# Causal attention and an MLP on one core: the score matmuls of a pair in one group, and another table of engines and ranks for the planner

## The chip, the cores and the metric

The kernel runs on one core of a Trainium2 chip. The time is the device time of one execution in us; smaller is better. A core has TensorE (PE, matmuls, with its weight loads shown apart as PEld), VectorE (DVE), ScalarE (ACT), GpSimd (POOL) and SyncE (SP), which here issues all DMAs. Each engine works through a queue of its own in order.

## The reference

```python
scores = q @ k.T / 8                      # q, k, v: 4 batches, 12 heads, 448 rows, 64 columns
scores = where(causal mask, -1e9, scores)
attn = exp(scores - max) / (sum + 1e-9)
x = (attn @ v) as (1792, 768)             # rows of all batches, heads side by side
h = x @ w_in                              # (768, 2048)
out = (h - tanh(h)) @ w_out               # (2048, 768)
```

The weights w_in and w_out come as 64-bit floats and are decoded on the chip.

## The kernel before, in words

**Numbers.** Nearly every operand of a matmul is split into two 16-bit parts, hi and lo, and three products (hi hi, hi lo, lo hi) are summed. `split` (L410) makes the parts: `scaled` (L396) writes hi = src * s, and a second step writes lo = src * s - hi. Either step can stand on VectorE (one pass for lo), or on GpSimd (for lo two passes: src scaled in place, then a subtraction); hi also on ScalarE.

**Stages.** (1) The first 128 rows of every batch are computed apart in `first_rows` (L595), with 32-bit matmuls: once for batches 0 and 1 (rank c0), once for batches 2 and 3 (rank c0b). (2) `w_in_chunk` (L445) loads and decodes w_in in 8 chunks. (3) `mlp_g` (L553) runs the MLP's first layer for these two groups of rows, 16 blocks of 18 matmuls each (`mlp1`, L519), chunk by chunk as w_in arrives; tanh on ScalarE, the rest of the eviction on VectorE, then a split into g. (4) `w_out_half` (L469) loads, decodes and splits the two halves of w_out. The second layer (`mlp2`, L535: 48 matmuls, one eviction o, one store) needs all of its half. (5) For each of the 4 batches `attention` (L735) computes the other 320 rows, and then the MLP runs on them. A batch has 6 pairs of heads. For a pair, `prep` (L654) loads q and k, bounds and splits q, k and v; query tile 0 has 256 keys, tile 1 has 384, and a last half tile of 64 rows has 448.

**Scores.** `weights_unit` (L684) handles one of the tiles 0 and 1 of a pair: 6 matmuls into two of four score banks (both heads, three products), for each head a VectorE pass that adds the mask and takes the minimum, an exponential on ScalarE with its sum, the reciprocal (`inverse`, L581), the split of the weights into p16 (tags p and p_lo, p_first for batch 0), and a DMA transpose into pT. `weights_last` (L702) does the same for the half tile, for two pairs at once. `values` (L723) multiplies with v: 54 matmuls for a pair into the bank b_x, which `split_x` empties into x. x has 9 buffers, so the attention can be three pairs ahead of the first layer of the batch before.

**Order.** Nothing is issued when it is written down: `Work` (L25 and on) collects all operations with the buffers that they touch, `schedule` (L159) lays them out by a list schedule with estimated costs (`cost`, L118) and waits, and `emit` (L228) issues them in order of their estimated start; so all instructions carry the line L232. Among the operations that an engine could start, the one with the lowest rank goes first. The ranks come from the table RANK; matmuls of the MLP have 10 and more, by batch and block. Operations that can stand on several engines are made by `either` (L107): its tag has a string in the table CFG, whose letters (V VectorE, A ScalarE, G GpSimd) are taken in turn. For example, "VAVV" for p puts three of four first halves of the weights on VectorE.

**The shared port.** The planner takes GpSimd's passes and some of VectorE's as users of one port, and doesn't let them overlap in its plan. In `add` (L70) VectorE's passes count if they read two large SBUF operands, or if they are a `tensor_scalar` with one, output of the same type and no scalar column.

**Buffers that tie the stages.** v of batch 0 lands where the x of the first rows was, and q and k of batch 0 land in the slot TS[4], which the second half of w_out uses last. The banks of the weights' decoding join the two score banks once w_out is done (`bank_s.bufs += banks[2:4]`).

## Time and profile before

| what | us |
|---|---|
| median of 3 runs (lowest, highest) | 605.71 (604.11, 606.19) |
| the profiled execution's own time | 603.75 |
| its span, first instruction to last | 602.0 |

A group of rows gives for each kind of instruction how often it ran, how long the engine was busy with it, the mean of one, and the idle time just before. The stretches are counted from the span's start. A busy TensorE means that matmuls overlap without a hole in the records; their ends are modelled. Names are the program's: b_s score banks, b_m the MLP's banks, b_x the banks of values, prob the exponentials, pn the split weights and pt their transposes, slot the large shared buffers, first a block that holds first rows, later g of batches 2 and 3, and later still second buffers of q, k, weights and exponentials.

### The profile page before, as it was taken

To read this page: it belongs to the slowest core of one execution; us is meant where nothing else is said; L and a number is where in the kernel's file an instruction comes from. 1 tells how busy PE (TensorE), PEld (TensorE's weight loads), DVE (VectorE), ACT (ScalarE), POOL (GpSimd) and SP (SyncE) were. 2 spreads that over 40 slices of the span, in tenths; PEclk is the share of its full clock that TensorE was granted. 3 is DMA by queue.
4 is the path that set the end of the run, shared out by engine and by line. 5 is a ranking of instruction groups with operands and counts; after the bars stand their busy time and mean duration, and the time that the engine had idled before them with its cause. 6 is when DMAs were issued, how large, how long until landed. Compare 5 with 4: busy or idle time off the path is not lost.

```text
span 602.0 us, 13635 instructions
## 1 busy us (share of the span) xinstructions
PE 559.2 (93%) x5144; PEld 375.9 (62%) x5144; DVE 451.6 (75%) x1286; ACT 294.8 (49%) x796; POOL 312.9 (52%) x389
## 2 busy tenths in 40 slices
PE   3688689999999999999999999999999999999997
PEld 3456468876555556765666666665666566776664
DVE  3889997989999999999959999921999961332000
ACT  5899899983366755553436463400644430121000
POOL 3577962883232157886528788510687820465000
PEclk9999899999999999999999999999999999999999
DMA  8995467645386974448563556640334281000100
GB/s 283 327 337 186 141 196 212 188 127 222 95 164 142 181 164 79 80 99 181 119 141 72 106 123 174 128 74 27 84 60 79 42 146 43 13 2 1 27 27 26
DMA packets 113378, 74.02 MB, mean 123 GB/s; under 512 B 89760, under 2 KB 99488, under 8 KB 112800
## 3 DMA queue, kind: packets, MB, share of 16 engines
q1 hardware_dynamic: 113312, 73.15, 48.8%
q8 instruction: 40, 0.66, 0.5%
q14 instruction: 26, 0.21, 0.1%
HBM read 45.61 MB, written 5.51 MB: 85 GB/s over the span
## 4 chain that ended last, share of the span: by engine, by line
PE 31%; DVE 31%; issue 3%; DMA 3%; POOL 3%; ACT 1%; DVEq 0%; SPq 0%; POOLq 0%; ACTq 0%
PE b_m L232 29%; DVE pn L232 6%; DVE prob L232 6%; DVE small L232 5%; DVE first L232 3%; DVE t L232 3%; DVE g L232 2%; PE b_x L232 2%; DVE v L232 2%; DVE k L232 1%; DMA e<-in_v_dram 1%; DVE x L232 1%; DMA slot<-in_qk_dram 1%; POOL g L232 1%; DMA pt<-pn 1%
## 5 line engine op out<-in xcount | busy, mean ns | idle before, releaser
L232 PE MATMUL b_m<-x,w_in 128*128 128x320 f16 (+1 forms) x1728 | 230.1, 291 | 15.3 <-DVE t L232 14.2
L232 PEld LDWEIGHTS <-w_in 128*128 128x128 f16 x1728 | 167.5, 98 | 72.1 <-issue 22.9
L232 PE MATMUL b_m<-slot,g 128*128 128x384 f16 x1152 | 192.4, 326 | 0.0
L232 PEld LDWEIGHTS <-g 128*128 128x128 f16 x1152 | 110.7, 98 | 74.9 <-issue 3.9
L232 ACT ACTIVATE prob<-prob,small 128x256 f32<-128x256 f32 (+2 forms) x102 | 58.8, 577 | 70.0 <-DVE small L232 69.5
L232 POOL TENSOR_SCALAR t<-t,small 128x320 f32<-128x320 f32 (+1 forms) x80 | 53.4, 668 | 51.6 <-DVE g L232 43.9
L232 ACT ACTIVATE t<-b_m,small 128x320 f32<-128x320 f32 (+1 forms) x96 | 48.1, 502 | 63.7 <-PE b_m L232 53.6
L232 DVE SCALAR_TENSOR_TENSOR t<-b_m,small,t 128x320 f32<-128x320 f32 (+1 forms) x96 | 49.9, 520 | 30.2 <-ACT t L232 30.0
L232 DVE TENSOR_SCALAR o<-b_m,small 128x384 f32<-128x384 f32 x28 | 17.1, 610 | 70.3 <-PE b_m L232 70.2
L232 POOL TENSOR_TENSOR g<-t,g 128x320 f16<-128x320 f32 x64 | 54.2, 847 | 5.3
L232 DVE CUSTOM_DVE_ANT_0 prob<-b_s,mask,small 128x384 f32<-128x384 f32 (+1 forms) x87 | 46.1, 545 | 0.2
L232 DVE SCALAR_TENSOR_TENSOR slot<-b_s,e 128x384 int32<-128x384 int32 x64 | 34.6, 547 | 5.5 <-ACT b_s L232 3.2
L232 DVE SCALAR_TENSOR_TENSOR pn<-prob,small,pn 128x256 f16<-128x256 f32 (+2 forms) x60 | 37.5, 645 | 0.1
L232 PEld LDWEIGHTS <-v 128*64 128x64 f16 x1296 | 31.5, 111 | 8.2 <-issue 8.0
L232 PE MATMUL b_m<-slot,first 128*128 128x384 f16 x192 | 33.6, 326 | 0.0
L232 PEld LDWEIGHTS <-first 128*128 128x128 f16 (+2 forms) x282 | 21.7, 98 | 17.6 <-issue 6.2
L232 PE MATMUL b_s<-k,q 64*128 64x256 f16 (+2 forms) x342 | 30.7, 317 | 0.4 <-DVE small L232 0.3
L232 ACT ACTIVATE e<-slot 128x768 f32<-128x768 f32 (+1 forms) x30 | 26.3, 876 | 5.4 <-DMA slot<-in_moe_w_in_dram 3.5
L232 POOL TENSOR_SCALAR prob<-prob,small 128x384 f32<-128x384 f32 (+2 forms) x24 | 15.4, 640 | 24.5 <-DVE pn L232 16.3
L232 DVE TENSOR_SCALAR g<-t,small 128x320 f16<-128x320 f32 x48 | 27.1, 564 | 0.4
L232 PE MATMUL b_x<-pt,v 128*64 128x64 f16 (+1 forms) x1026 | 26.3, 207 | 0.3 <-DMA pt<-pn 0.3
L232 DVE TENSOR_SCALAR small<-small 128x1 f32<-128x1 f32 (+4 forms) x159 | 26.0, 178 | 0.2
(137 smaller groups left out, 815.9 us busy)
## 6 DMA issues: line engine op xcount, KB each, us to landing
slot<-in_moe_w_in_dram SPq DMA_DIRECT2D x16, 768.0 KB, 6.2
slot<-in_qk_dram SPq DMA_DIRECT2D x18, 384.0 KB, 3.3
slot<-in_moe_w_out_dram SPq DMA_DIRECT2D x8, 768.0 KB, 4.7
e<-in_moe_w_out_dram SPq DMA_DIRECT2D x8, 768.0 KB, 4.5
e<-in_v_dram SPq DMA_DIRECT2D x3, 1536.0 KB, 6.6
out_dram<-o SPq DMA_DIRECT2D x24, 192.0 KB, 1.9
first<-in_qk_dram SPq DMA_DIRECT2D x6, 384.0 KB, 3.4
g<-in_qk_dram SPq DMA_DIRECT2D x6, 256.0 KB, 6.5
```

Of the source, the lines that this page charges most:

```text
L232: getattr(self.eng[o["eng"]], method)(*args, **kw)
```

## The change

It has four parts. `weights_units` replaces `weights_unit`: at tile 0 all 12 matmuls of the pair's tiles 0 and 1 are issued as one group into four score banks, and the passes on tile 1 use the banks later. `split` gets a third way for lo: ScalarE scales src in place and GpSimd subtracts; and the two passes of GpSimd's way become two operations of the plan. The plan's costs and its port change: every VectorE `tensor_scalar` with one large SBUF input and no PSUM operand counts as a user, an operation may start 190 or 135 ns before the port is free, the port stays taken 75 or 22 ns longer, some passes of ScalarE cost 75 ns more and GpSimd's subtraction 20 ns. And the tables CFG and RANK are other ones: of the ranks, c0b goes from 9.316 to -12.684, evac from 4.208 to -4.596, w_out from 7.476 to -4.564, att from -0.165 to -7.342, w_in from -12.778 to -17.446, c0 from -14.292 to -74.72, att0 from -13.314 to -11.803.

```diff
@@ -97,23 +97,28 @@
         if eng == "G":
             shared = bool(ins)
         else:
-            two_ports = method == "tensor_scalar" and len(big) == 1 and outs[0].dtype == big[0].dtype and len(ins) == 1
+            two_ports = method == "tensor_scalar" and len(big) == 1 and not any(x.space == bass.MemoryType.PSUM for x in outs + ins)
             shared = eng == "V" and (len(big) > 1 or two_ports)
         op.setdefault("shared", set()).update([eng] if shared else [])
         cost, move = self.cost(eng, method, outs, ins)
         total[0] += cost
         op["move"] += move
 
-    def either(self, tag, *ways):
+    def either(self, tag, *ways, again=False, A="A"):
 
         self.ops.append(dict(alts={}, deps=set(), rank=self.rank, move=0.0))
         self.alt = True
         for f in ways:
             f()
         self.alt = None
-        n = self.turn[tag] = self.turn.get(tag, -1) + 1
-        way = CFG[tag]
-        self.ops[-1].update(eng=way[n % len(way)], tag=(tag, n))
+        n = self.turn[tag] = self.turn.get(tag, -1) + (not again)
+        way = CFG[tag].replace("A", A)
+        self.ops[-1].update(eng=way[n % len(way)], tag=(tag, n), A=A)
+
+    def nothing(self, eng):
+        self.ops[-1]["alts"][eng] = [], [0.0]
+        self.ops[-1].setdefault("shared", set())
 
     def cost(self, eng, method, outs, ins):
         o = max(outs, key=lambda x: x.size())
@@ -135,10 +140,11 @@
             b = o.size() * mybir.dt.size(o.dtype)
             return 540.0, b / (360.0 if run >= 512 else 180.0)
         if eng == "A":
-            return n * 0.833 + (51 if psum else 94) + 93 * aps + 93 * (len(outs) > 1), 0.0
+            words = ins[0].space != bass.MemoryType.PSUM and (o.space == bass.MemoryType.PSUM or ins[0].ap[-1][0] > 1)
+            return n * 0.833 + (51 if psum else 94) + 93 * aps + 93 * (len(outs) > 1) + 75 * (words and not aps), 0.0
         if eng == "G":
             if method == "tensor_tensor":
-                return n * 1.885 + 148, 0.0
+                return n * 1.885 + 168, 0.0
             return n * 0.83 + 245, 0.0
         if method in ("tensor_scalar", "tensor_copy") and not psum and not any(st == 0 for x in ins for st, m in x.ap[1:] if m > 1):
             return n * 0.52 + 70 + 60 * aps, 0.0
@@ -179,7 +185,8 @@
                 heapq.heappush(ready[e], (self.ops[i]["rank"], i))
             _, i = heapq.heappop(ready[e])
             o = self.ops[i]
-            if e in o["shared"] and port > t:
+            lead = 190.0 if e == "V" else 135.0
+            if e in o["shared"] and port - lead > t:
                 other = [x for x in ready[e] if e not in self.ops[x[1]]["shared"]]
                 if other:
                     heapq.heappush(ready[e], (o["rank"], i))
@@ -200,8 +207,8 @@
                 else:
                     turn, mode = self.TURN, o["mode"]
             if e in o["shared"]:
-                t = max(t, port)
-                port = t + o["cost"]
+                t = max(t, port - lead)
+                port = t + o["cost"] + (75.0 if e == "V" else 22.0)
             o["start"] = t
             end = t + turn + o["cost"]
             if e == "T":
@@ -219,7 +226,7 @@
             for j in users[i]:
                 left[j] -= 1
                 f = self.ops[j]["eng"]
-                at[j] = max(at[j], end + (self.SAME if f == e else self.LAT)[f])
+                at[j] = max(at[j], end + (self.LAT[f] if f != e else self.SAME[f] if o["cost"] else 0.0))
                 if not left[j]:
                     heapq.heappush(waiting[f], (at[j], j))
         self.span = max(free.values())
@@ -409,12 +416,11 @@
 
     def split(hi, lo, src, s, tag):
 
-        def lo_pool():
-            G.tensor_scalar(src, src, s, 1.0, ALU.mult, ALU.mult)
-            G.tensor_tensor(lo, src, hi, ALU.subtract)
-
         scaled(hi, src, s, tag)
-        wk.either(tag + "_lo", lambda: V.scalar_tensor_tensor(lo, src, s, hi, ALU.mult, ALU.subtract), lo_pool)
+        wk.either(tag + "_lo", lambda: wk.nothing("V"), lambda: G.tensor_scalar(src, src, s, 1.0, ALU.mult, ALU.mult),
+                  lambda: A.activation(src, src, AF.Copy, scale=s))
+        wk.either(tag + "_lo", lambda: V.scalar_tensor_tensor(lo, src, s, hi, ALU.mult, ALU.subtract),
+                  lambda: G.tensor_tensor(lo, src, hi, ALU.subtract), again=True, A="G")
@@ -681,23 +687,27 @@
         S.dma_start_transpose(out=pT.rearrange("p x a t q -> p (x a t) q"), in_=p16.rearrange("p x a k -> p (x a k)"))
         return pT
 
-    def weights_unit(b, o, i):
-        w = W[i]
+    def weights_units(b, o, n):
+        if n == 0:
+            o.pS = [[bank_s() for _ in range(2)] for _ in range(2)]
+            with wk.group():
+                for i in range(2):
+                    w = W[i]
+                    for m, (x, y) in enumerate(HL):
+                        for h, half in enumerate(halves):
+                            T.matmul(o.pS[i][h][:, :w], o.q[half, x, i * P:(i + 1) * P], o.k[half, y, :w], start=(m == 0), stop=(m == 2))
+        w = W[n]
         total, mn = r_sum(), r_mn()
-        pS = [bank_s(), bank_s()]
-        with wk.group():
-            for n, (x, y) in enumerate(HL):
-                for h, half in enumerate(halves):
-                    T.matmul(pS[h][:, :w], o.q[half, x, i * P:(i + 1) * P], o.k[half, y, :w], start=(n == 0), stop=(n == 2))
         es = [e_ring()[:, :w] for _ in range(2)]
         for h in range(2):
-            softmax_part(es[h], pS[h][:, :w], mask[:, 3 * P - w:], o.cn, mn[:, h:h + 1], total[:, h:h + 1])
+            softmax_part(es[h], o.pS[n][h][:, :w], mask[:, 3 * P - w:], o.cn, mn[:, h:h + 1], total[:, h:h + 1])
         inverse(total, 2.0 ** -14)
-        p16 = p16_rings[i]()
+        p16 = p16_rings[n]()
         for h in range(2):
             split(p16[:, h, 0, :], p16[:, h, 1, :], es[h], total[:, h:h + 1], tag(b, "p"))
-        o.pT[i] = transposed(i, p16)
+        o.pT[n] = transposed(n, p16)
 
     def weights_last(b, os):
 
@@ -751,7 +761,7 @@
             for u, o in enumerate(os):
                 for i in range(2):
                     at(hp + u)
-                    weights_unit(b, o, i)
+                    weights_units(b, o, i)
                     if i == 0 and hp + U + u < NP:
                         nxt.append(prep(b, hp + U + u, vf[:, hp + U + u], sv))
             at(hp + U - 1)
@@ -823,8 +833,8 @@
         wk.emit()
 
 
-CFG = {"early": 4, "e_bufs": 4, "b_out": "A", "b_qk": "AAV", "shift_in": "AGG", "inverse": "A", "w_in": "AVGA", "w_in_lo": "GGV", "shift_out": "AVAG", "w_out": "VAAA", "w_out_lo": "V", "p0": "G", "p0t": "AVAA", "x0": "VVVAAV", "g0": "GGGA", "g0_lo": "V", "g2": "GVVV", "g2_lo": "G", "g": "VVGV", "g_lo": "G", "o": "V", "k_first": "VAVGGA", "k_first_lo": "VVGV", "q_first": "G", "q_first_lo": "V", "v_first": "GVA", "v_first_lo": "V", "p_first": "AGGAVA", "p_first_lo": "V", "k": "GVGG", "k_lo": "V", "q": "VA", "q_lo": "G", "v": "GVAV", "v_lo": "GVV", "p": "VAVV", "p_lo": "VGV", "x": "AAVA"}
-RANK = {"c0": -14.292, "w_in": -12.778, "evac": 4.208, "w_out": 7.476, "c0b": 9.316, "att0": -13.314, "att": -0.165}
+CFG = {"early": 4, "e_bufs": 4, "b_out": "V", "b_qk": "VAAAVV", "shift_in": "AGV", "inverse": "AVVAAV", "w_in": "VAGV", "w_in_lo": "GGVA", "shift_out": "GGA", "w_out": "GAA", "w_out_lo": "AVVV", "p0": "G", "p0t": "AVVVAV", "x0": "AVV", "g0": "GAG", "g0_lo": "A", "g2": "AAG", "g2_lo": "GVVA", "g": "VVVA", "g_lo": "GVGG", "o": "AAV", "k_first": "VGVV", "k_first_lo": "VGGAAA", "q_first": "AAVVVG", "q_first_lo": "VGVV", "v_first": "AGA", "v_first_lo": "VVAA", "p_first": "AGA", "p_first_lo": "V", "k": "AV", "k_lo": "AAVV", "q": "AGVV", "q_lo": "AAVVAA", "v": "VVGVAV", "v_lo": "AGA", "p": "AAG", "p_lo": "VAVAGV", "x": "AVA"}
+RANK = {"c0": -74.72, "w_in": -17.446, "evac": -4.596, "w_out": -4.564, "c0b": -12.684, "att0": -11.803, "att": -7.342}
 
 
 _OUTS = [((1792, 768), "float32")]
```

## Rows read from the trace of the kernel before

**Rows 1.** The page's first line and its part 1: the span, and for each engine its busy time in us, the share of the span and the number of instructions.

```profile
span 602.0 us, 13635 instructions
PE 559.2 (93%) x5144; PEld 375.9 (62%) x5144; DVE 451.6 (75%) x1286; ACT 294.8 (49%) x796; POOL 312.9 (52%) x389
```

**Rows 2.** The table by stretch of the whole program. Columns: the stretch in us from the span's start, its length, the busy us of each engine with its number of instructions, TensorE's granted clock as a share of full speed, the share of the DMA engines, GB/s.

```profile
0.00:40.00 40.00, 23.41 (x132) 16.83 (x132) 26.22 (x117) 30.61 (x88) 22.96 (x25) 1.00 0.95 317
40.00:60.00 20.00, 17.37 (x162) 13.63 (x163) 18.05 (x82) 19.27 (x47) 13.88 (x10) 1.00 0.66 215
60.00:80.00 20.00, 12.59 (x106) 9.91 (x104) 18.80 (x66) 17.77 (x41) 15.82 (x13) 0.91 0.44 138
80.00:150.00 70.00, 66.69 (x561) 53.15 (x559) 64.05 (x137) 56.13 (x119) 41.83 (x52) 1.00 0.63 195
150.00:270.00 120.00, 116.66 (x1210) 73.18 (x1209) 117.75 (x347) 67.83 (x210) 59.82 (x81) 1.00 0.60 126
270.00:310.00 40.00, 39.52 (x368) 24.06 (x368) 34.87 (x89) 15.02 (x45) 22.15 (x28) 1.00 0.73 156
310.00:380.00 70.00, 67.73 (x791) 45.73 (x786) 68.26 (x197) 37.15 (x111) 52.91 (x70) 1.00 0.49 111
380.00:420.00 40.00, 40.00 (x339) 24.75 (x337) 14.47 (x32) 5.49 (x14) 9.13 (x11) 1.00 0.42 80
420.00:488.00 68.00, 65.07 (x640) 42.80 (x639) 65.68 (x180) 35.51 (x106) 49.15 (x66) 1.00 0.37 71
488.00:602.00 114.00, 110.19 (x861) 71.84 (x858) 23.50 (x47) 9.98 (x19) 25.28 (x38) 0.99 0.14 31
```

**Rows 3.** The chain that ended last: its shares of the span by engine (the page's part 4), and from the same chain in order of time its longest piece (start us, us, what).

```profile
PE 31%; DVE 31%; issue 3%; DMA 3%; POOL 3%; ACT 1%; DVEq 0%; SPq 0%; POOLq 0%; ACTq 0%
...
503.62 94.82 PE b_m L232 x630
```

**Rows 4.** The waits, one row: who waited for whom, us in total, how often, the longest in us.

```profile
PE b_m L232 <- DVE t L232: 14.2, 17, 2.5
```

**Rows 5.** Instructions of TensorE in order of time, merged where they follow one another: start us, us, operation, count. The matmuls that write scores of tiles 0 and 1.

```profile
177.53 0.99 PE L232 MATMUL b_s<-k,q 64*128 64x256 f16 x12
...
279.59 0.50 PE L232 MATMUL b_s<-first 64*128 64x256 f16 x6
285.01 0.66 PE L232 MATMUL b_s<-first 64*128 64x384 f16 x6
...
470.88 0.99 PE L232 MATMUL b_s<-k,q 64*128 64x256 f16 x12
```

**Rows 6.** Groups of VectorE's instructions. Columns: line, engine, operation, out<-in, partitions x elements, count | busy us, mean ns of one | idle us before them and what ended it. The first two rows are grouped over shapes, with the number of other forms.

```profile
L232 DVE TENSOR_SCALAR pn<-prob,small 128x384 f16<-128x384 f32 (+2 forms) x41 | 20.8, 518 | 0.1
L232 DVE SCALAR_TENSOR_TENSOR pn<-prob,small,pn 128x256 f16<-128x256 f32 (+2 forms) x60 | 37.5, 645 | 0.1
...
L232 DVE SCALAR_TENSOR_TENSOR v<-e,small,v 128x512 f16<-128x512 f32 x12 | 10.6, 881 | 0.1
L232 DVE SCALAR_TENSOR_TENSOR k<-slot,small,k 128x448 f16<-128x448 f32 x14 | 12.0, 857 | 0.0
L232 DVE TENSOR_SCALAR o<-b_m,small 128x384 f32<-128x384 f32 x28 | 17.1, 610 | 70.3 <-PE b_m L232 70.2
L232 DVE SCALAR_TENSOR_TENSOR q<-slot,small,q 128x320 f16<-128x320 f32 x6 | 3.2, 538 | 0.0
L232 DVE TENSOR_SCALAR small<-small 128x1 f32<-128x1 f32 x78 | 12.5, 173 | 0.1
L232 DVE TENSOR_REDUCE small<-first 128x1 f32<-128x448 f32 x6 | 3.6, 605 | 0.0
L232 DVE CUSTOM_DVE_ANT_0 prob<-b_s,mask,small 128x384 f32<-128x384 f32 x48 | 28.5, 605 | 0.2
```

**Rows 7.** Groups of ScalarE's and GpSimd's instructions, the same columns.

```profile
L232 ACT ACTIVATE pn<-prob,small 128x384 f16<-128x384 f32 x10 | 6.0, 610 | 10.1 <-DVE small L232 10.1
L232 ACT ACTIVATE q<-slot,small 128x320 f16<-128x320 f32 x3 | 1.7, 562 | 5.5 <-DVE small L232 5.5
L232 ACT ACTIVATE small<-small 128x2 f32<-128x2 f32 x57 | 11.1, 196 | 0.9
...
L232 POOL TENSOR_SCALAR t<-t,small 128x320 f32<-128x320 f32 x64 | 40.5, 633 | 47.5 <-DVE g L232 43.9 <-DVE small L232 2.7
L232 POOL TENSOR_TENSOR g<-t,g 128x320 f16<-128x320 f32 x64 | 54.2, 847 | 5.3
```

**Rows 8.** VectorE's pass that makes the first half of g, in the view of the tile g (operation, count, duration in ns at least / median / at most, first and last start in us, forms) and as a group with the columns of rows 6.

```profile
L232 DVE TENSOR_SCALAR g<-t,small x48: 371/427/1005, 231.2 to 552.9; 128x320 f16<-128x320 f32 x48
...
L232 DVE TENSOR_SCALAR g<-t,small 128x320 f16<-128x320 f32 x48 | 27.1, 564 | 0.4
```

**Rows 9.** What SyncE issued, in order of time: start us, us, what. The first load of the first rows of batches 2 and 3, and the first loads of q and k for the attention of batch 0.

```profile
16.43 0.48 SPq L232 DMA_DIRECT2D slot<-in_qk_dram  x1
...
149.93 1.26 SPq L232 DMA_DIRECT2D slot<-in_qk_dram  x2
```

**Rows 10.** From the views of the tiles g and pn, with the columns of rows 8: the second layer's matmuls on the tile g (first start 136.5 us), and the mask passes of the first rows; and the group of the one reduction of 1536 columns on a slot, with the columns of rows 6.

```profile
L232 PE MATMUL b_m<-slot,g x1152: 326/326/337, 136.5 to 598.1; 128*128 128x384 f16 x192
L232 DVE CUSTOM_DVE_ANT_0 pn<-b_s,mask x48: 256/284/292, 5.2 to 84.3; 128x128 f32<-128x128 f32 x48
...
L232 DVE TENSOR_REDUCE small<-slot 128x1 f32<-128x1536 f32 x1 | 1.8, 1753 | 1.1 <-DMA slot<-in_v_dram 1.1
```

## The prediction

> **What bounds the kernel now.** I read the page's totals first [rows 1]. The span of the profiled execution is 602.0 us, and TensorE is busy in 559.2 of them. So all that any order of the work can win, with these matmuls, lies in the 42.8 us in which TensorE idles, and in pauses hidden inside its busy time. VectorE is busy for 451.6 us, ScalarE for 294.8, GpSimd for 312.9.
>
> The table by stretch [rows 2] says where those 42.8 us lie. The reader should subtract the PE column from the length of each stretch: 16.6 us of idle in 0:40, where the DMA share is 0.95 (the loads), 2.6 in 40:60, 7.4 in 60:80, 3.3 in 80:150; that is 29.9 before 150. From 150 to 488, where the attention of the four batches runs beside the MLP, it idles 3.3 + 0.5 + 2.3 + 0.0 + 2.9 = 9.0 us out of 338. After 488 it is 3.8, nearly all behind the last matmul. In that middle part VectorE is as full as TensorE: 117.8 of 120, 68.3 of 70, 65.7 of 68, against only 14.5 of 40 in 380:420. The chain of waits agrees [rows 3]: 31% of the span is TensorE and 31% VectorE, and it ends with 630 matmuls in 94.82 us (151 ns each, without a gap). The waits name how VectorE holds TensorE up [rows 4]: TensorE waited 14.2 us in 17 places for the VectorE pass that empties an MLP bank.
>
> So from 150 on two engines are full at once. VectorE is what can be relieved; TensorE's 9.0 us of idle are what the relief can turn into time.
>
> **The change, part by part.** The sum is made against the profiled execution's own 603.75 us, which lies 1.96 us under the median of 605.71; I add that back at the end.
>
> *The score group.* A pair's twelve matmuls for tiles 0 and 1 become one group. In the trace such matmuls already stand together: for 18 of the 24 pairs they run as one row of 12 in 0.99 us, the first of these at 177.53 and the last at 470.88; a pair that is split takes 0.50 + 0.66 us [rows 5]. Joining the six others saves 0.17 us each and a return to the MLP's matmuls that no row prices; at the least 0, at most another 0.66 for each, so 0 to 4 in all. I take 6 x 0.17 = 1.0, what the rows show. The change also adds a wait: the group needs all four score banks free, so behind it on TensorE's queue the MLP's matmuls stand until the fourth bank has been read. Who reads it is the VectorE mask pass, 605 ns [rows 6]. Where VectorE has slack that wait hides behind MLP matmuls placed ahead of the group; without it, it is up to one such pass for each pair, 24 x 0.6 = 14 us. I take 0, because the 12 already run together in 18 pairs, so the old order met the same wait.
>
> *Engines of the attention and of the MLP (the table of turns).* Counting turns from the two tables: VectorE gives up all 72 first halves of the weights (p, p_first; 518 ns in the mean of the shapes, 37 us in all), 15 of the second halves (645 ns, 9.7), 12 of v_lo (881 ns, 10.6), 10 of k_lo (857 ns, 8.6), 19 of 28 output evictions (610 ns, 11.6), and on balance 4.4 for k, q and v of batch 0. It takes on 16 second halves of g (538 ns, the SBUF pass of the same 320 columns: 8.6), 8 bounds of q and k (605 ns for 448 columns, so at most 4.8), 32 of the small sums before the reciprocal (173 ns, 5.5), 6 q_lo (3.2), and some 4 us of first halves of k, v and x [rows 6]. Net: 82 given up, 26 taken on, some 57 us less VectorE in a part where it was busy for 301.
>
> ScalarE takes most of it: 42 more first halves of p and p_first at about 0.6 us (25), 30 scalings in place for p_lo (18), 34 for k, q and v (23), 16 first halves of g (562 ns, 9), 19 outputs (at the price of the same pass, 10), less 8 bounds (5.5) and 32 sums (196 ns, 6.3): some 75 us more [rows 7], on 161 us in 150:488 [rows 2]. GpSimd loses 16 of the 64 second halves of g (633 + 847 ns each), the 16 first halves that it made and the scaling passes of q_lo, and gains 30 of p and the subtractions behind ScalarE's scalings: by count some 5 us less than the 193 that it has there. So after the change the middle part holds VectorE 244, ScalarE 236, GpSimd 188 of 338 us: none over 72% where VectorE had 89%. What is late next is then TensorE itself.
>
> What that is worth: the 9.0 us of idle, at most. Of these I take 6.5. Not all, because the pauses are short (17 waits that sum to 14.2 us over the whole program) and the same bank now waits for ScalarE's tanh, in whose queue some 75 us of copies now stand; each may hold it by one copy of 0.6 us.
>
> *The order counts VectorE's SBUF passes on the port.* The planner now holds VectorE's one-input passes and GpSimd's apart. The row shows what there is to hold apart: the pass that makes g's first half takes 371 ns at the least and 1005 at the most [rows 8], 564 in the mean, so 48 x 0.19 = 9.3 us of VectorE time for that group. It is VectorE time, between 0 and 9.3; with VectorE no longer full I count it at 0 in the span, since the 57 us have freed it already.
>
> *Before 150.* Here the ranks change: the first rows of batches 2 and 3 (c0b) move ahead of the MLP evictions and of the decoding of w_out, in all queues, SP's and GpSimd's among them. Their loads go out from 16.43 us on already [rows 9], behind w_in, and stay behind it in rank. SP loses nothing by it. The engines: VectorE gains the 16 bounds of w_out (between the reductions of 448 columns, 605 ns, and of 1536, 1753 ns: 0.94 each, 15) and smaller things (14), and gives up 16 + 12 + 4 + 4 + 4 others (24.7): 5 us more. ScalarE has about 6 less, GpSimd about 6 more, of 64.1, 56.1 and 41.8 busy us in 80:150. The stage ends for the attention when w_out is decoded, since batch 0's q and k land in a slot that w_out's second half uses: SP issues them at 149.93 [rows 9]. Worst case, the 5 us stand in full at that point; best case, the 7.4 us of idle in 60:80 go, because both chunks' first MLP layer is ready to run beside w_in. I take a gain of 1, for the fullest engine gets 5 more and the hole 7.4 less, and the two nearly cancel.
>
> *The tail.* From 503.62 on the matmuls run back to back; the last eviction moves to ScalarE at nearly the same price. 0.
>
> **The sum**: 603.75 - 1.0 - 6.5 - 1 = 595.25; plus 1.96 for the median, 597.2 us.
>
> **A rule of the skill.** In 488:602 TensorE runs without gaps and its weight loads are busy in 71.84 of 114 us, 63% [rows 2]; the whole span has 62% [rows 1]. So 62% is full for this mix. The Trainium skill, in Perfetto Trace Analysis, section Identifying the Most-Contended Engine, would have TensorE judged by the busy share of its weight loads and not by its matmuls, and the other engines by occupancy; by that, VectorE with 75% is the one to relieve and TensorE has room. The trace speaks against this reading here, and its price is the third rival.
>
> **The rivals.**
>
> *The cover fails before 150 (slower).* c0b's first rows go ahead of w_out. On VectorE they are half of the 48 mask passes (11.6 us), half of 8 and 12 evictions, one reduction, some 17 us; now they fill holes until 84.3 us and beyond [rows 10]. If they push the decoding of w_out back by all of that but some 4 us that still find holes, the first matmul of the second layer, now at 136.5, starts near 150, while the first layer has run dry. TensorE then idles some 13 us more and the attention starts as much later; the middle part gives its 7 back, and the time is 605.7 + 13 - 7 = 612, or about 608 if half of it is hidden. It decides if that matmul starts after 143. For it: VectorE is busy for 64 of 70 us in 80:150. Against: the total work is nearly the same, and work that stands earlier is not there later. 0.22.
>
> *The relief is taken back (no change).* TensorE waits as long for ScalarE's tanh as it waited for VectorE, and each split over two engines makes the way from score to transpose longer; the 9.0 us stay. Time 604 to 607. 0.15.
>
> *VectorE is the only bound.* Its 31% of the chain are 187 us; shorter by 57/301 they would win 35 us, for 570. Against it: TensorE has only 9.0 us of idle there to give. 0.02. It is how the section of the Trainium skill named above would have it.
>
> **How the numbers follow.** Forecast 0.61, with 597.2 inside a range of its own from 588 to 603.9; the three rivals 0.22, 0.15 and 0.02. The measurement tells some 0.3%, 1.8 us, from no change. Faster by more than that: 0.61 + 0.02 = 0.63; within it 0.15; slower 0.22. The low end takes the other 2.5 of the 9.0, the other 3 of the groups and half of the 7.4 in 60:80: 597.2 - 2.5 - 3 - 3.7 = 588. The high end takes in the half-hidden case of the first rival: 610.
>
> **What would show it.** Right: VectorE's busy time near 395 us and ScalarE's near 364; TensorE's idle in the attention part down to 2 or 3 us while its busy time stays near 559; the chain nearly all TensorE behind 150; score runs of 12 for all 24 pairs. Wrong: the first second-layer matmul after 143, a new wait of TensorE for ScalarE's tanh beyond 10 us, or VectorE still near 99% busy beside the MLP's first layer.

## The result, and the profile of the changed kernel

The change makes the kernel **slower**: 613.80 us (median of 4 runs, 611.27 to 614.17) against 605.37 (604.11 to 606.19), a ratio of 1.0137 with a 95% interval of 1.0111 to 1.0163. The forecast was 597.2 with a range up to 610, so it has the wrong sign and lies outside its range. The profiled execution took 613.75 us. Of the five executions of e3 below the profiled one took 1157.48 us, with 562 ns for each matmul of 384 columns instead of 326; e3's time is the median of its other four, and nothing is read from its trace.

The page's first line and the busy times of the engines, beside [rows 1]:

```profile
span 612.0 us, 13704 instructions
PE 565.1 (92%) x5144; PEld 379.8 (62%) x5144; DVE 422.1 (69%) x1225; ACT 355.1 (58%) x886; POOL 307.0 (50%) x371
```

VectorE did lose work (451.6 to 422.1 us) and ScalarE gained it (294.8 to 355.1), yet the span grew by 10.0 us: TensorE idles 46.9 us where it idled 42.8, and is busy 5.9 us longer with the same 5144 matmuls (2.8 of these 5.9 in the first layer of the first rows, 68.1 to 70.9 us, the rest in many small groups). The table by stretch, with the columns of [rows 2], says where:

```profile
0.00:40.00 40.00, 21.00 (x115) 15.25 (x115) 26.88 (x105) 27.17 (x76) 18.84 (x20) 1.00 0.95 314
40.00:60.00 20.00, 15.64 (x107) 11.12 (x109) 16.65 (x77) 14.48 (x34) 7.58 (x5) 0.91 0.61 197
60.00:80.00 20.00, 13.56 (x120) 10.36 (x116) 19.51 (x86) 19.68 (x58) 18.50 (x14) 0.89 0.26 82
80.00:150.00 70.00, 66.06 (x567) 55.12 (x566) 63.04 (x131) 56.14 (x112) 48.58 (x62) 0.98 0.67 211
150.00:270.00 120.00, 117.88 (x1214) 73.58 (x1213) 112.70 (x343) 87.44 (x234) 64.18 (x78) 1.00 0.65 130
270.00:310.00 40.00, 38.59 (x392) 23.76 (x391) 37.12 (x110) 28.98 (x78) 29.01 (x37) 1.00 0.68 157
310.00:380.00 70.00, 65.57 (x755) 42.64 (x751) 68.39 (x186) 55.24 (x150) 51.68 (x65) 1.00 0.71 142
380.00:420.00 40.00, 38.73 (x458) 24.19 (x460) 35.71 (x104) 32.52 (x85) 31.66 (x40) 1.00 0.63 113
420.00:488.00 68.00, 67.72 (x563) 46.11 (x564) 22.58 (x53) 17.17 (x39) 18.83 (x28) 1.00 0.18 40
488.00:602.00 114.00, 114.00 (x841) 74.01 (x840) 19.54 (x39) 15.71 (x29) 18.19 (x28) 1.00 0.05 15
```

Three things are to be seen. **Before 150** TensorE idles 33.7 us instead of 29.9, and in 40:60 ScalarE (14.48) and GpSimd (7.58) idle with it, where before they had 19.27 and 13.88 busy us. **From 150 to 488** TensorE idles 9.5 us, as before (9.0). **VectorE's relief lies in the wrong place**: up to 420 it is fuller than before (112.70 + 37.12 + 68.39 + 35.71 = 253.9 of 270 us, against 235.4), and only in 420:488 it is nearly free (22.58 against 65.68), where the last scores are done (they end at 420.7 us) and TensorE runs nearly without a gap anyway.

The early loss in three views. The tiles g and w_in (duration at least / median / at most, first and last start) give the second layer's start, 136.5 before [rows 10], and the last maximum over w_in, which started at 73.7 before:

```profile
L239 PE MATMUL b_m<-slot,g x1152: 323/326/337, 144.7 to 608.1; 128*128 128x384 f16 x192
...
L239 PE MATMUL b_scales<-w_in,ones x48: 272/273/421, 19.8 to 83.1; 128*128 128x256 bf16 x48
```

TensorE's groups in 40:80, first the changed kernel and then the kernel before (count | busy us, mean ns):

```profile
L239 PE MATMUL b_m<-x,w_in 128*128 128x256 f16 x76 | 12.8, 326 | 1.1 <-DVE x L239 0.9 <-DVE t L239 0.2
```

```profile
L232 PE MATMUL b_m<-x,w_in 128*128 128x256 f16 x140 | 18.1, 279 | 7.7 <-DVE t L232 6.9 <-DVE small L232 0.6 <-DVE x L232 0.3
```

64 matmuls of the first layer fewer are done there, and the record of each is 47 ns longer in the mean, at a granted clock of 0.91 and 0.89 instead of 1.00 and 0.91 [rows 2].

What TensorE waits for in 160:500 (us in total, times, longest): its largest row before, then its largest rows in the changed kernel; and the chain that ended last there, beside [rows 3]:

```profile
PE b_m L232 <- DVE t L232: 4.7, 8, 1.0
```

```profile
PE b_s L239 <- DVE small L239: 2.1, 3, 1.1
PE b_x L239 <- DVE x L239: 1.9, 5, 0.7
PE b_scales L239 <- DVE small L239: 1.8, 5, 0.5
PE b_m L239 <- DVE t L239: 1.6, 4, 0.8
```

```profile
PE 30%; DVE 18%; ACT 5%; issue 4%; DMA 3%; POOL 2%; DVEq 0%; POOLq 0%; ACTq 0%
...
425.76 62.63 PE b_m L239 x432
...
493.12 115.29 PE b_m L239 x756
```

The wait that the forecast meant to remove (b_m for VectorE's t) is down from 4.7 to 1.6 us there; the other 9.5 of the 14.2 us in [rows 4] lie outside this stretch. In its place the attention's own matmuls wait for VectorE: scores, values and maxima, 5.8 us where it was 2.4.

### The profile page after: what moved, and what is told of

It is laid out like the page before. It is cut to its first block, busy times and chain, and to the rows that moved or that the text cites. A ratio compares the mean times of both kernels' runs of the same rounds, so it can differ in the third digit from the quotient of the medians.

```text
span 612.0 us, 13704 instructions
## 1 busy us (share of the span) xinstructions
PE 565.1 (92%) x5144; PEld 379.8 (62%) x5144; DVE 422.1 (69%) x1225; ACT 355.1 (58%) x886; POOL 307.0 (50%) x371
## 4 chain that ended last, share of the span: by engine, by line
PE 30%; DVE 18%; ACT 5%; issue 4%; DMA 3%; POOL 2%; DVEq 0%; POOLq 0%; ACTq 0%
PE b_m L239 29%; DVE small L239 5%; DVE prob L239 3%; DVE first L239 2%; DVE pn L239 2%; DVE t L239 2%; DVE g L239 2%; ACT prob L239 1%; DMA e<-in_v_dram 1%; DVE k L239 1%; DVE q L239 1%; DMA slot<-in_qk_dram 1%; DVE x L239 1%; ACT first L239 1%; PE b_x L239 1%
## 5 line engine op out<-in xcount | busy, mean ns | idle before, releaser
L239 POOL TENSOR_SCALAR t<-t,small 128x320 f32<-128x320 f32 (+1 forms) x52 | 30.2, 580 | 118.4 <-DVE g L239 106.7
L239 ACT ACTIVATE prob<-prob,small 128x384 f32<-128x384 f32 (+2 forms) x126 | 71.0, 569 | 16.4 <-DVE small L239 15.6
L239 ACT ACTIVATE o<-b_m,small 128x384 f32<-128x384 f32 x19 | 10.9, 573 | 92.5 <-PE b_m L239 92.5
L239 DVE TENSOR_SCALAR o<-b_m,small 128x384 f32<-128x384 f32 x9 | 5.5, 614 | 79.9 <-PE b_m L239 79.9
L239 POOL TENSOR_TENSOR g<-t,g 128x320 f16<-128x320 f32 (+1 forms) x64 | 50.3, 788 | 7.6 <-ACT t L239 4.7
L239 DVE CUSTOM_DVE_ANT_0 prob<-b_s,mask,small 128x256 f32<-128x256 f32 (+1 forms) x87 | 45.6, 547 | 1.7 <-POOL pn L239 1.4
L239 DVE TENSOR_SCALAR small<-small 128x1 f32<-128x1 f32 (+4 forms) x197 | 42.8, 233 | 5.0 <-ACT pn L239 2.3
L239 ACT ACTIVATE slot<-slot,small 128x768 f16<-128x768 f32 (+4 forms) x35 | 27.2, 791 | 11.2 <-DVE first L239 4.0
L239 ACT ACTIVATE pn<-prob,small 128x256 f16<-128x256 f32 (+2 forms) x50 | 27.3, 574 | 4.4 <-DVE small L239 3.3
L239 POOL TENSOR_TENSOR v<-e,v 128x512 f16<-128x512 f32 x18 | 21.7, 1205 | 11.0 <-ACT e L239 10.9
```

The costliest lines, as they stand in the source:

```text
L239: getattr(self.eng[o["eng"]], method)(*args, **kw)
```

## The experiments

Ratios are to the kernel before on the same chip, with their intervals. Two theories stood against each other. **Relief**: less VectorE work turns into TensorE time, and something else in the change takes it back. **Order**: VectorE's load was not what made TensorE idle; the tuned order was.

**The four parts alone** (e1 to e4). Each is put by itself into the kernel before:

```diff
-                    weights_unit(b, o, i)
+                    weights_units(b, o, i)        # e1
...
+            lead = 190.0 if e == "V" else 135.0   # e2: the port's rules and the prices
...
-CFG = {"early": 4, "e_bufs": 4, "b_out": "A", ...
+CFG = {"early": 4, "e_bufs": 4, "b_out": "V", ...   # e3: new table, with the split in three steps
...
-RANK = {"c0": -14.292, ...
+RANK = {"c0": -74.72, ...                         # e4
```

> The kernel before with the score group alone; tables, ranks and plan as before. All theories of the loss (A: the new ranks put the first rows of batches 2 and 3 ahead of the decoding and delay it; B: the new table of engines makes the decoding stage longer) expect 604 to 606 us and the first second-layer matmul near 136.5. A rival, C: the group's wait for four banks holds TensorE's queue, then 608 to 614 and more than 5 us of new waits of TensorE in front of score matmuls. A second rival, D: any reordering moves the time by about 1% either way, then a change of over 3 us without one place to show for it.

> The kernel before with the plan's port rule and costs of the change alone; no group, old table, old ranks. A and B expect 603 to 607 us. If the plan's new port rule is itself the loss, 610 to 615, with VectorE's one-input passes no shorter than in the kernel before (g's first half 564 ns in the mean); if the rule works, that mean falls below 450 ns. D: over 3 us either way.

> The kernel before with the new table of engines and the third way of the split alone; old ranks, old plan, no group. A expects a gain: 597 to 602 us, first second-layer matmul at 134 to 138, VectorE near 420 us busy. B expects the loss: 610 to 615, with that matmul after 142.

> The kernel before with the new ranks alone; old table, old plan, no group. A expects the loss: 610 to 615 us, with the first second-layer matmul after 142 and the end of the decoding of w_in after 90 (84.3 before). B expects 603 to 607 and 136.

Measured: e1 607.81 us (1.0044 [1.0023, 1.0064]), e2 621.21 (1.0260 [1.0217, 1.0302]), e3 625.15 (1.034 [1.030, 1.038]), e4 625.90 (1.0358 [1.0309, 1.0406]). Each part alone is slower than before, and three of them are slower than all four together. The costs don't add, so none of the parts has a price of its own. What was expected fell short each time: e1 lies between its ranges, e2 to e4 above every range given. The loss of e2 begins ahead of the attention: its order ends the decoding of w_out at 177.9 us, where it ended at 150.8 before.

**Early and late apart** (e5 to e8). These kernels hold both versions and change over where w_out has been decoded; e5 is old until there and new behind it, e6 the other way round. e7 is e5 with the old ranks behind that point too, e8 is e6 with c0b ranked behind evac and w_out again, as it was before.

```diff
+    wk.early, wk.old = True, True     # e5, e7: ahead of the first rows; e6, e8: True, False
     rank(RANK["c0"])
     c = new_chunk(2 * P)
...
+    wk.early, wk.old = False, False   # e5, e7; e6, e8: False, True
     for x in (c, c2):
         o_scale(x)
...
-"evac": -4.596, ... "att0": -11.803, "att": -7.342     # e5
+"evac": 4.208, ... "att0": -13.314, "att": -0.165      # e7
...
-"c0b": -12.684     # e6
+"c0b": 0.0         # e8
```

> A kernel in two phases, planned in one schedule. Phase one, all until w_out is decoded (first rows, both weights, first layer of the first rows), has the table, ranks, plan rule and split of the kernel before, and the order of its instructions is that of the kernel before up to some 125 us. Phase two, the attention and the MLP on it, is all new, with the score group. If the loss is made before 150 (E), the first second-layer matmul is back at 136.5 and the time falls by 6 to 9 us from 613.8, to 605 to 608. If it is made in the attention part (F), it stays at 612 to 616 although that matmul comes at 136.5. If the relief of VectorE pays there once phase one no longer eats it (G, the forecast's own claim), 596 to 601.

> The converse: phase one all new, in the order of the changed kernel up to some 150 us; phase two with the old table, ranks, plan rule, split, and no score group. E expects 611 to 615, with the first second-layer matmul near 144.7. F expects 604 to 607. G expects 618 to 622, as the old attention part lacks the relief.

> As the run with the old phase one and the new phase two, but with the old ranks of the attention and of the evictions (att, att0, evac). If it is the new rank, which puts all matmuls of the attention ahead of all of the MLP, that makes TensorE wait in its queue for them (H), TensorE's idle in 160:500 before b_s, b_scales and b_x falls from about 7 us to below 4 and the time is 3 to 5 us lower than in that run. If the rank is not it, the two agree within 2 us.

> As the run with the new phase one and the old phase two, but with the rank of the first rows of batches 2 and 3 (c0b) back behind the evictions and w_out (0.0 in place of -12.684). If it is c0b's place that delays phase one (A), the first second-layer matmul comes at 136 to 139 and the time falls by 5 to 8 us from that run. If it is the new table of engines or the plan's rule (B), that matmul stays at 143 or later.

Measured: e6 611.12 (1.0085 [1.0059, 1.0110]) with the second layer from 144.1: the early part alone costs 5 to 6 us. e5 611.38 (1.0109 [1.0086, 1.0132]): the late part alone costs 6 as well, though its early part is the old one (second layer from 136.1). e7 607.71 (1.0041 [1.0024, 1.0059]): 3.7 of these 6 are the new ranks, though the waits ahead of scores, values and maxima, which were to fall below 4 us, only fell from 10.7 to 7.5. e8 620.07 (1.0234 [1.0192, 1.0276]), second layer at 154.2: with c0b back in its old place the early part gets 9 us worse, and w_out is decoded at 169.7 us instead of 160.1. So beside the other new parts c0b's new place is not what delays it.

The table by stretch shows what the new ranks do to VectorE; e5 (new ranks), then e7 (old ranks):

```profile
310.00:380.00 70.00, 67.41 (x753) 44.85 (x753) 65.75 (x201) 56.63 (x152) 53.94 (x67) 1.00 0.67 135
380.00:420.00 40.00, 38.88 (x543) 24.70 (x541) 30.93 (x95) 31.77 (x84) 30.88 (x39) 1.00 0.80 123
420.00:488.00 68.00, 68.00 (x528) 45.97 (x528) 18.66 (x39) 12.17 (x23) 15.88 (x24) 1.00 0.11 28
```

```profile
310.00:380.00 70.00, 67.92 (x668) 44.63 (x668) 59.98 (x178) 49.04 (x131) 45.55 (x59) 1.00 0.48 105
380.00:420.00 40.00, 39.76 (x427) 25.48 (x422) 11.84 (x26) 12.61 (x31) 15.47 (x18) 1.00 0.42 86
420.00:488.00 68.00, 66.91 (x699) 44.54 (x698) 55.09 (x162) 46.93 (x126) 43.17 (x57) 1.00 0.41 77
```

The same work: with the new ranks it is pressed into the time up to 420, with the old ones it is spread. e7 puts att, att0 and evac back together; that it is att is read from the code. The MLP of batch b has ranks from 10 + b (first layer) to 10.75 + b (second). The pairs hp = 0 to 5 of batch b + 1 have att + 10 + b + hp / 6: with the old ranks 9.84 + b to 10.67 + b, pair by pair among those layers; with the new ones 2.66 + b to 3.49 + b, ahead of every matmul of the MLP.

**Relief without handing over** (e9). The order, the engines and the instructions of before; only VectorE's passes for the softmax weights work on 64 columns once their buffer has been written in full.

```diff
+                if o.get("tag", ("",))[0] in ('p', 'p_first', 'p_lo', 'p_first_lo'):
+                    key = args[0].tensor.name, args[0].offset
+                    if key in full and o["eng"] == "V":
+                        args = [x[:, :64] if isinstance(x, bass.AP) and x.size() > x.shape[0] else x for x in args]
+                    full.add(key)
```

> The kernel before with every instruction in its old place on its old engine; only VectorE's passes that write the two halves of the softmax weights work on 64 columns instead of 256 to 512 once their buffer has been written in full (so most of the weights are left over from an earlier pair: this part of the computation is changed). VectorE loses some 45 to 60 us of work, about the relief that the forecast counted, and nothing is handed to another engine or reordered. Theory R (the forecast's step: VectorE's load is what makes TensorE idle between 150 and 488 us, relief turns into TensorE's time): 4 to 7 us faster than before, 598 to 601, TensorE's idle in 160:500 down from 8.3 to 1 to 4. Theory O (the idle comes from where the old list puts the work and from chains that pass over several engines, VectorE's load is not what ends the waits): within 2 us of before, idle still 7 to 9.

Measured: 594.46 us, ratio 0.9803 [0.9782, 0.9824], 11.6 us faster. The page's totals, the middle of the table by stretch, and all waits of TensorE in 160:500:

```profile
span 593.0 us, 13635 instructions
PE 557.1 (94%) x5144; PEld 376.3 (63%) x5144; DVE 413.4 (70%) x1286; ACT 295.0 (50%) x796; POOL 301.5 (51%) x389
```

```profile
150.00:270.00 120.00, 118.33 (x1229) 74.69 (x1227) 108.18 (x354) 69.50 (x213) 60.18 (x84) 1.00 0.60 126
270.00:310.00 40.00, 40.00 (x409) 24.51 (x408) 28.40 (x86) 13.69 (x42) 19.15 (x26) 1.00 0.77 160
310.00:380.00 70.00, 69.32 (x765) 46.68 (x762) 64.77 (x210) 39.11 (x115) 52.15 (x74) 1.00 0.61 119
...
420.00:488.00 68.00, 68.00 (x696) 45.35 (x693) 53.04 (x168) 33.79 (x99) 47.12 (x68) 1.00 0.50 92
```

```profile
PE b_scales L238 <- DVE small L238: 0.7, 1, 0.7
PE b_m L238 <- DVE t L238: 0.6, 2, 0.3
```

38 us less VectorE, TensorE's idle in 150:488 from 9.0 to 2.4 us. In the order of before, Relief holds and Order falls: VectorE's load is what makes TensorE idle there. The idle fell by 6.6 us, as the forecast took it. The time fell by more than was expected (598 to 601), as busy times fell too with the same instructions: TensorE's from 559.2 to 557.1 us, GpSimd's from 312.9 to 301.5.

**Halves of the early part, and a mere reshuffle** (e10 to e12). e10 has in the early part the new table and split on the old ranks and rules; e11 the new ranks and rules on the old table; late all old. e12 changes 1 ns of the planner:

```diff
+    wk.early, wk.old, wk.thirds = True, True, True      # e10; e11: True, False, False
...
+    wk.early, wk.old, wk.thirds = False, True, False    # e10, e11
...
-    TURN = 100.0
+    TURN = 101.0                                        # e12
```

> Until w_out is decoded: the new table of engines with the new split in three steps, but the old ranks and the old planner's rules; behind that everything as before. Run e6 (everything new in this stretch) was 5.7 us slower than before with the second layer starting at 144.1. Theory T (the table sends the early work to the wrong engines: 15 us of bounds of w_out to VectorE): 4 to 8 us slower, second layer at 142 to 147. Theory R (the new ranks and the planner's rules make the loss): within 2 us of before, second layer at 136 to 138. Theory M (the parts only work together): over 8 us slower, second layer after 147.

> Until w_out is decoded: the old table of engines, but the new ranks and the new planner's rules; behind that everything as before. Theory R (the new ranks and rules make the early loss): 4 to 8 us slower than before, second layer at 142 to 147. Theory T (the new table makes it): within 2 us of before, second layer at 136 to 138. Theory M (the parts only work together, each is fitted to the others): over 8 us slower, second layer after 147.

> The kernel before with one number of the planner changed by 1 ns (what it counts for a change of TensorE's mode: 101 instead of 100), so that the same work on the same engines with the same ranks is put in another order here and there. It measures what a mere reshuffle does. Theory O (the order before is a tuned point; any other order of the same rules costs some us): 2 to 10 us slower than before. Theory B (a reshuffle alone moves the time by less than can be measured, so that the loss of the change needs a part of its own): within 1.8 us of before.

Measured: e10 626.72 (1.0341 [1.0314, 1.0368]), second layer at 158.6; e11 634.34 (1.0468 [1.0444, 1.0492]), at 144.3, and w_out decoded at 177.9 instead of 150.8. Theory M holds by the times (its sign, a second layer after 147, came in e10 alone): each half by itself costs 21 to 28 us, both together (e6) 6. e12 605.46 (0.9988 [0.9972, 1.0003]): its order differs on every engine from some 235 us on, and nothing comes of it. So not every other order is worse; one made by the same rules, tables and ranks cost nothing.

**What ends the waits in the changed kernel** (e13, e14, e16). Its order and engines stay; the edit is that of e9, for ScalarE's passes (e13) or VectorE's (e14), and in e16 for the 16 bounds of w_out:

```diff
-                    if key in full and o["eng"] == "V":     # e14
+                    if key in full and o["eng"] == "A":     # e13
...
+                if o.get("tag", ("",))[0] == "b_out" and o["eng"] == "V":   # e16
+                    args = [args[0], args[1][:, :64]]
```

> The changed kernel (613.8 us) with every instruction in its place; ScalarE's passes for the two halves of the softmax weights work on 64 columns once their buffer has been written in full (most of the weights are then left over: this part of the computation is changed). ScalarE loses an estimated 30 to 45 us, more than half of what the change gave it. Theory S (the copies handed to ScalarE take the relief back: results come later, buffers and banks stay full): 6 to 12 us faster than the changed kernel, 602 to 608. Theory V (VectorE still ends the waits): 2 us or less, 612 to 614. Theory O (the order alone): 612 to 614.

> As e13, but VectorE's remaining passes for the weights work on 64 columns (an estimated 20 to 30 us less VectorE; ScalarE and GpSimd as in the changed kernel; this part of the computation is changed). Theory V (VectorE, still 113 of 120 us busy in 150:270, still ends the waits): 5 to 10 us faster than the changed kernel, 604 to 609. Theory S (ScalarE's copies): 2 us or less, 612 to 614. Theory O (the order alone): 612 to 614.

> The changed kernel with every instruction in its place; the 16 bounds of w_out on VectorE look at 64 columns of 768 each (the scale of w_out comes from a part of it: this part of the computation is changed). VectorE loses an estimated 10 to 12 us between 80 and 150. Theory B (the forecast's item: these bounds are what VectorE has too much before 150): w_out decoded some 8 us earlier than 160.1, 3 to 8 us faster than the changed kernel. Theory W (the early loss is made before 84, where w_in is decoded and TensorE has too little to do): 2 us or less, 612 to 614, the second layer still starts after 143.

Measured: e14 605.62 (0.9996 [0.9972, 1.0021]), 8 us faster than the changed kernel for 18.6 us less VectorE; e13 611.03 (1.0096 [1.0071, 1.0121]), some 2.5 us faster for 21 us less ScalarE, between the ranges of its theories (the intervals leave 0 to 5 us); e16 612.33 (1.0117 [1.0071, 1.0164]), not to be told from the changed kernel, for 8.7 us less VectorE before 150, with w_out decoded at 158.2 instead of 160.1. Theory V holds: VectorE still ends most of the waits, and the weights' passes that were handed to ScalarE take back little. A cut pass also shortens the way from score to transpose; but e13 cuts that way about as much as e14 and gains a third of it, so the gain is VectorE's load in the main. The bounds of w_out are not the early loss.

```profile
PE 563.9 (93%) x5144; PEld 380.5 (63%) x5144; DVE 403.5 (67%) x1225; ACT 355.2 (59%) x886; POOL 298.5 (49%) x371
```

This is e14's page.

**The handing over alone** (e17). The kernel before with two entries of the new table:

```diff
-"p_first": "AGGAVA", ... "p": "VAVV"
+"p_first": "AGA", ... "p": "AAG"
```

> The kernel before with two entries of the table of engines taken from the change: the first halves of the softmax weights, p and p_first, go to ScalarE and GpSimd (some 37 us off VectorE); ranks, planner and the rest as before. Theory H (the handing over itself pays where nothing else is changed, nearly as e9's relief): 596 to 602. Theory S (ScalarE and GpSimd take it back): 604 to 608. Theory T (tables and ranks are fitted to each other, one entry changed disturbs the list): 610 to 625, as in e2 to e4.

Measured: **598.07 us**, ratio 0.9877 [0.9844, 0.9910]. This kernel beats both. Its totals and its middle part:

```profile
span 597.2 us, 13683 instructions
PE 558.6 (94%) x5144; PEld 376.1 (63%) x5144; DVE 424.1 (71%) x1214; ACT 314.9 (53%) x838; POOL 328.3 (55%) x419
```

```profile
150.00:270.00 120.00, 118.17 (x1224) 74.14 (x1223) 114.27 (x337) 74.67 (x225) 62.18 (x88) 1.00 0.62 128
270.00:310.00 40.00, 39.68 (x359) 24.06 (x357) 28.55 (x75) 16.39 (x46) 24.14 (x31) 1.00 0.65 154
310.00:380.00 70.00, 68.68 (x805) 46.73 (x803) 60.00 (x168) 41.22 (x118) 54.97 (x75) 1.00 0.53 112
380.00:420.00 40.00, 39.47 (x342) 24.28 (x340) 16.43 (x39) 7.54 (x22) 13.11 (x16) 1.00 0.34 75
420.00:488.00 68.00, 68.00 (x702) 44.70 (x699) 59.23 (x164) 42.65 (x120) 55.61 (x78) 1.00 0.40 78
```

VectorE is busy 424.1 us here and 422.1 in the changed kernel: the totals are alike, the times are 16 us apart. Here the relief lies in every stretch in which VectorE was full (219.3 us up to 420, against 235.4 before and 253.9 in the changed kernel), and TensorE idles 4.0 us in 150:488.

**What lies between e17 and e7** (e18, e19). Both have the old early part and the old ranks. e18 has all entries of the new table and the split behind w_out, but the old rules and no score group; e19 has only the entries p and p_first, with the new rules and the group.

```diff
+    wk.early, wk.old, wk.thirds = True, True, False     # e18, e19
...
+    wk.early, wk.old, wk.thirds = False, True, True     # e18
+    wk.early, wk.old, wk.thirds = False, False, False   # e19, with weights_units
```

> Until w_out is decoded all as before; behind that the whole new table of engines with the split in three steps, but the old ranks, the old planner's rules and the scores of a tile by itself. Run e17 (two entries of the table) gave 598.1, run e7 (this kernel with the planner's rules and the score group) 607.7. Theory P (the planner's rules and the group spoil it): 596 to 601. Theory K (the table's other entries spoil it: k, q, v, outputs, small sums): 605 to 610. Both in part: 601 to 605.

> Until w_out is decoded all as before; behind that the two entries p and p_first of e17 with the new planner's rules (port and prices) and the score group, other entries and ranks as before. Theory P (the planner's rules and the group spoil it): 605 to 610. Theory K (the table's other entries): 596 to 601. Both in part: 601 to 605.

| us | old rules, no group | new rules and group |
|---|---|---|
| entries p, p_first | 598.07 (e17) | 615.65 (e19) |
| all entries, split | 606.90 (e18) | 607.71 (e7) |

Ratios: e18 1.0018 [1.0001, 1.0036], e19 1.0164 [1.0140, 1.0189], above every range that was given for it. Both halves spoil e17's gain, the rules and the group by 17.6 us, the other entries with the split by 8.8, and not as a sum: with all entries the rules and the group cost 0.8. e19 loses it between 150 and 270, where TensorE idles 11.7 us:

```profile
150.00:270.00 120.00, 108.28 (x1119) 67.72 (x1118) 106.89 (x317) 67.60 (x201) 54.40 (x75) 0.97 0.58 122
```

e18 is the nearest test of the forecast's main step: the table and the split behind w_out, and nothing else. It gains nothing. In 150:488 (columns of [rows 2]), e17 and then e18:

```profile
150.00:488.00 338.00, 334.00 (x3422) 213.91 (x3421) 278.49 (x778) 182.48 (x529) 210.01 (x286) 1.00 0.53 111
150.00:488.00 338.00, 327.35 (x3364) 209.70 (x3362) 269.35 (x785) 217.40 (x574) 189.55 (x241) 0.99 0.52 111
```

VectorE has 9.1 us less to do in e18 than in e17, and less up to 420 too (213.5 us against 219.3), yet TensorE idles 10.7 us instead of 4.0. What TensorE waits for in 160:500 of e18:

```profile
PE b_m L242 <- DVE t L242: 3.5, 4, 2.5
PE b_x L242 <- DVE x L242: 2.4, 3, 0.9
PE b_scales L242 <- DVE small L242: 1.7, 2, 1.4
PE b_m L242 <- DVE x L242: 1.6, 1, 1.6
PE b_m L242 <- ACT o L242: 1.1, 2, 0.7
```

The waits still end with VectorE, 9.2 us of these 10.3, though it has less to do. So its busy time alone, by stretch too, does not say how long TensorE waits; when its passes come matters as well. Which of the other entries spoil it, or whether the split does, no run shows.

## Why the prediction was wrong

**What bounds the kernel** was right for the order of before. TensorE's idle in the middle comes from VectorE's load there, as e9 shows by 11.6 us, and e17 by 7.4 with a real table. But of the 14.2 us of [rows 4] that I took as a sign of it only 4.7 lie in 160:500.

**The relief step** ("of these I take 6.5") is the step that failed. It takes VectorE's busy time off the middle and lets TensorE's idle follow, as if the new table changed nothing else. With the table and the split alone behind w_out (e18) VectorE is down from 301.0 to 269.4 of 338 us, TensorE's idle is 10.7 us instead of 9.0, and the time is 1 us longer than before instead of 6.5 shorter. The other entries of the table, with the split, take e17's gain away. In the changed kernel the new ranks cost 3.7 us more (e5 against e7): I had the load spread over 338 us, VectorE at 72%. It has 276.5 us there, 82%, and 253.9 of the 270 us up to 420, 94%. I looked at the ranks only before 150 and priced att at nothing.

**The sum of the parts**, from run to run and by the medians, is this: the early part 5.7 us (e6), the table behind w_out 1.0 (e18), rules and group there 0.8 (e7 against e18), ranks there 3.7. That is some 11 us, and 8.4 were measured; they don't add up exactly.

**The amount** of relief was too high too: busy time 422.1 instead of near 395. My count was near: taken with the mean durations of before, the changed counts come to some 50 us less, against my 57 less 5. But the passes that stayed got longer by some 12 us in all, most of it in the small sums and scales, of which I priced 32 more at 173 ns [rows 6]. Before and after:

```profile
L232 DVE TENSOR_SCALAR small<-small 128x1 f32<-128x1 f32 (+4 forms) x159 | 26.0, 178 | 0.2
```

```profile
L239 DVE TENSOR_SCALAR small<-small 128x1 f32<-128x1 f32 (+4 forms) x197 | 42.8, 233 | 5.0 <-ACT pn L239 2.3
```

The rest is that neighbouring records overlap, and busy time counts an overlap once: the records sum to 38.0 us less, the busy time to 29.5. ScalarE's 355.1 was near my 364.

**The port rule** ("0 in the span") had no row for its price. I asked what the port costs the passes [rows 8], not what the rule does to the order: e2, with the rules and prices alone, is 16 us slower, and e19, with rules and group, 17.6 slower than e17. Beside the whole table they cost 0.8 us behind w_out (e7 against e18), so the changed kernel lost little by them there; what they do before 150 beside the other parts is not shown.

**The score group** (a gain of 1, its wait 0) went the other way: alone it costs 2.7 us (e1). In 160:500 its score matmuls wait 2.4 us for VectorE's small results, instead of 1.5.

**Before 150** (a gain of 1) was a loss of 5 to 6 (e6), the second large term that failed. "SP loses nothing by it" was wrong: c0b's eight loads are all issued by 30.1 us, not 41.9, and w_in's last load lands at 70.2, not 64.9. But that is not shown to be the cause, since c0b's old place makes it worse (e8). The balance "the fullest engine gets 5 more and the hole 7.4 less" failed as a method: in 40:60 every engine idled more, so no engine's sum bounded that stretch. The bounds on VectorE are not the cause (e16), and either half of the change by itself costs more than both (e10, e11). What makes the 5 us stays open.

**The first rival** was right in sign and in its test (144.7, past 143; e13 and e16, with the same order, had 141.9 and 142.9), and by luck in its figure of 612. Its 17 us of VectorE were too many: half of the 48 mask passes, at the 284 ns of [rows 10], is 6.8 us and not 11.6. Its mechanism, c0b's work pushing back w_out, does not hold: in e8, with c0b behind w_out, w_out is decoded later (169.7 us against 160.1 in e6) and not earlier. The loss of the late part was not in its view. **The second rival** (the relief is taken back) has its outcome in e18, 606.9 us in its 604 to 607, but not its mechanism: of TensorE's waits there 1.1 us end with ScalarE, and less work for ScalarE on the weights gains some 2.5 us (e13). **The third** doesn't arise: 38 us less VectorE gave 11.6 us (e9) and not the 23 or so that its price (35 for 57) implies. Of the Trainium skill's rule in Perfetto Trace Analysis, Identifying the Most-Contended Engine, the runs show that the share has to be read against its value at full work: the weight loads are busy 60% of the span in the slowest of these kernels (e11), 63% in the fastest (e9), and 65% in a stretch where the matmuls run without a gap (74.01 of 114 us in 488:602 of the changed kernel). So 62% was near full here, but not full, as the prediction had it.

**The tail** was right at 0: 756 matmuls run without a gap to the end.

## What to carry to other kernels

Relief of a full engine pays where it holds up the bound, so compare its busy time stretch by stretch and not by its total. But busy time does not price a change of table even so: e17 and e18 lie within 5 us of each other in every stretch of 150:488, and their times are 8.8 us apart. Where a planner orders the work, a new table, rank, price or rule is a change of the whole order and has no price from rows; bound it by tens of us on both sides, and try the one part that has a mechanism (here two entries of the table, 7.4 us) by itself. Work cut short in a frozen order (e9, e14) measures what an engine's load is worth before anyone looks for another engine to take it.

## What was not expected of the hardware

With their instructions in the same order, and the same up to there, the changed kernel and e13, e14, e16 ended w_in's maxima at 83.4, 80.7, 84.5 and 82.2 us, with granted clocks in 40:60 of 0.91, 0.86, 0.74 and 0.74. So an early point of one profile is worth some 2 us either way, and a clock of that stretch tells nothing alone. From 270 to 488 it stood at 1.00 in all of them.
